# A new table of instruction orders for a fused attention, Fourier and feed-forward kernel

## The chip, the core and the metric

The kernel runs on one core of a Trainium2 chip. A core has four compute engines that run side by side, each its own list of instructions in order: TensorE (PE, with its weight loads PEld), VectorE (DVE), ScalarE (ACT) and GpSimd (POOL). SyncE (SP) issues the DMA transfers. An instruction waits until the semaphores of what it needs have come; what stands behind it on its engine waits too. The metric is the device time of one execution in microseconds (us).

## What is computed

Attention runs over 4 batches, 8 heads, 768 tokens of 64 values. A query sees only keys that belong to the same of 16 clusters as itself. The result goes through a two-dimensional Fourier transform, of which the real part is added, a normalisation, and a feed-forward layer of width 2048.

```python
q_assign = np.argmax(np.einsum('bhsd,hcd->bhsc', q_n, c_n), axis=-1)
k_assign = np.argmax(np.einsum('bhsd,hcd->bhsc', k_n, c_n), axis=-1)
mask = q_assign[:, :, :, None] == k_assign[:, :, None, :]
scores = scale * np.matmul(q, k.transpose(0, 1, 3, 2))
scores = np.where(mask, scores, -1000000000.0)
scores = scores - np.max(scores, axis=-1, keepdims=True)
attn = np.exp(scores)
attn = attn / (np.sum(attn, axis=-1, keepdims=True) + 1e-09)
return np.matmul(attn, v).astype(np.float32)
...
x = np.ascontiguousarray(attn_out.transpose(0, 2, 1, 3)).reshape(B, S, H * D)
...
X = np.fft.fft(x, axis=1)
X = np.fft.fft(X, axis=2)
mixed = np.real(X).astype(np.float32)
u = x + mixed
mu = np.mean(u, axis=-1, keepdims=True)
var = np.mean((u - mu) ** 2, axis=-1, keepdims=True)
un = (u - mu) / np.sqrt(var + 1e-06)
ch = np.maximum(un @ w_ch1, 0.0) @ w_ch2
return (u + ch).astype(np.float32)
```

## The kernel before

Numbers are kept as pairs of 16-bit values, a high and a low part, so that one product takes three matmuls. The work is recorded in steps. A pair of heads (there are 16) has six steps of 128 queries; in a step each of the two heads has the following chain. PE forms the scores in a PSUM bank, `ps_big`, of which there are two, one a head (L538 for the first eight pairs, with the mask's matmuls L543 behind; L530 for the others). DVE scales them and takes the row's smallest negated value (L557). ACT takes the exponential (L560) and casts it to 16 bits (L568; in some steps POOL does, L566). POOL subtracts to get the low part (L569). SP transposes both parts with a DMA (L571) into the ring `pts`. Two steps later PE multiplies them with v (L589 to L591, `ps_o`), and DVE divides by the sums (L601, L603, L605). In the first pairs of batch 0 L557 writes to SBUF, so the bank is free when L557 ends; later it writes in place, and the bank is free when L560 ends.

Some steps ahead of its first score a pair is prepared: loads, the split of q and k (ACT L397, DVE L398) and of v (ACT L361, DVE L363), the matmuls with the cluster centres (L425, four column strips of 32), the choice of the cluster (ACT L428, PE L433, DVE L439, L441, L447 to L458) and the mask.

Beside the first batch the two weight matrices are read in 32 pieces, their largest value is found (L725, L728, L62 to L65) and they are split (ACT L744, L745, PE L754, DVE L758, ACT L764, L767, DVE L770 or POOL L768). When a batch's attention is done its Fourier transform follows: folds on DVE and POOL (L892, L915, L928), their split (ACT L897, DVE L899), matmuls (L991 and others), and then the feed-forward layer (up: L1286, ACT L1293 and L1294, POOL L1295; down: L1314, DVE L1318), beside the attention of the next batch.

What stands where on an engine is set by a table. The program is recorded, and at the end `Order.apply` takes each engine's instructions, unpacks that engine's string from `ORDERS`, which holds how far each instruction moves from the place where it was recorded, sorts by it and ties every instruction to the one before it. What an instruction needs from another engine it still waits for by semaphore, wherever it stands. The tables were found beforehand; the kernel itself decides nothing.

Of the kernel before, what the change touches and what calls it, by code (L numbers as in the profile page):

```python
# [32 lines left out]
SH = S // 2  # L33
# [34 lines left out]
class Counted:  # L68
# [5 lines left out]
    def tile(self, shape, dt, name, bufs=None, **kw):  # L74
# [28 lines left out]
    "SP": (
        "c-lRaX>J=a427wYW{I7xNl?@U3KT`}&=d5GJxcGApK*{P>1MaiOzp9U{Yc3f!&)fn@$r!gGHDR|^4Q6!gGNcRXRM{y8f(RG#j2I)UZV=Dz;DvE&Z"
        "WWjORwdi8OQ9sPI_8=M(##O%->&5qHOT~q3_u5Jj#}R?YEPA4chq_9KUBi0n3<K^hpo8a}SF!<2-Xt@~jn}8+|2fP0rphI*(I1g5Wi&;n-<L$hfw"
# [118 lines left out]
class Attention:  # L224
# [23 lines left out]
    VP = ()  # L248
# [1340 lines left out]
```

## Time and profile before

| what | value |
|---|---|
| timed runs | 949.96, 950.37, 955.26 us (median 950.37) |
| span of the profiled execution, first to last instruction | 949.3 us |
| PE busy | 863.9 us, 91% |
| DVE busy | 678.2 us, 71% |
| ACT busy | 601.6 us, 63% |
| POOL busy | 608.3 us, 64% |
| mean granted TensorE clock | 0.976 of 2.4 GHz |

The profile is one execution. Busy is the time in which an engine had an instruction running; a PE that is busy runs at the full clock of 2.4 GHz or at half of it, 1.2 GHz, which the clock column tells (1.00 is full). In the timeline a row is one instruction or a run of equal ones, with its start in us from the span's start, its duration, and, where the engine sat idle before it, for how long and what ended that. Names read out<-in; L557 is line 557 of the kernel before.

### The profile page before, as it was taken

The page shows a single profiled execution, that of the slowest core. Times are in us where ns is not written, and L with a number is a line of the kernel's source. Part 1 is how long each engine was busy: PE and PEld are TensorE (multiplying, and loading weights), DVE is VectorE, ACT ScalarE, POOL GpSimd, SP SyncE. Part 2 cuts the span into 40 slices and gives each one's busy share as a digit, 9 for nine tenths or more (in the row PEclk, how much of TensorE's full clock was granted, in tenths as well). Part 3 has the DMA queues.
Part 4 walks back from the last instruction along what each step waited for, and adds up shares of the span by engine and source line. Part 5 has one row for each costly group of instructions (what it writes and reads, how often), then busy time and mean ns, then how long its engine had stood idle before and what let it go on. Part 6 is the DMA issues. An engine that isn't in the chain of part 4 may idle for free.

```text
span 949.3 us, 23660 instructions
## 1 busy us (share of the span) xinstructions
PE 863.9 (91%) x9241; PEld 581.0 (61%) x9241; DVE 678.2 (71%) x1531; ACT 601.6 (63%) x944; POOL 608.3 (64%) x752
## 2 busy tenths in 40 slices
PE   4777776677999999998999999999999999999998
PEld 1334443345756748666758667667668586676674
DVE  7989888877756667677757567678773446889643
ACT  6989988776666747647757747657676563353320
POOL 3778786755876876746767768748677764342421
PEclk9999897889999999999999999999999999999999
DMA  9999999988588888999899889998887764201020
GB/s 360 242 217 192 233 262 222 224 169 159 103 169 144 146 178 164 184 177 173 157 171 184 174 155 187 197 173 187 151 147 153 132 118 101 60 1 41 19 78 23
DMA packets 405151, 150.20 MB, mean 158 GB/s; under 512 B 383024, under 2 KB 391728, under 8 KB 405040
## 3 DMA queue, kind: packets, MB, share of 16 engines
q1 hardware_dynamic: 404896, 148.67, 78.1%
q8 instruction: 72, 1.18, 0.5%
q14 instruction: 39, 0.32, 0.1%
q10 hardware_dynamic: 144, 0.03, 0.0%
HBM read 41.99 MB, written 6.29 MB: 51 GB/s over the span
## 4 chain that ended last, share of the span: by engine, by line
PE 56%; DMA 7%; DVE 5%; POOL 4%; ACT 4%; issue 2%; SPq 1%; ACTq 0%; POOLq 0%; DVEq 0%
PE ps_fb L1314 8%; PE ps_fc L1314 7%; DMA pts<-ph 7%; PE ps_fa L1286 6%; PE ps_fa L1314 5%; PE ps_fb L1286 5%; PE ps_fc L1286 5%; PE ps_big L530 5%; PE ps_big L1228 3%; POOL ph L569 2%; PE ps_o L589 2%; PE ps_o L590 2%; PE ps_o L591 2%; PE ps_big L538 1%; ACT ph L568 1%
## 5 line engine op out<-in xcount | busy, mean ns | idle before, releaser
L569 POOL TENSOR_TENSOR ph<-p,ph 128x768 f16<-128x768 f32 x144 | 238.4, 1656 | 112.8 <-ACT ph L568 96.8
L557 DVE TENSOR_SCALAR_CACHE_REDUCE ps_big<-ps_big,sce 128x768 f32<-128x768 f32 x144 | 145.4, 1020 | 60.5 <-PE ps_big L530 34.7
L1314 PEld LDWEIGHTS <-arena 128*128 128x128 f16 x1152 | 109.9, 98 | 121.4 <-issue 1.6
L560 ACT ACTIVATE p<-ps_big,rmx 128x768 f32<-128x768 f32 x144 | 128.7, 897 | 60.3 <-DVE ps_big L557 43.0
L568 ACT CAST ph<-p 128x768 f16<-128x768 f32 x144 | 119.6, 830 | 70.0 <-DMA pts<-ph 67.7
L1295 POOL TENSOR_TENSOR arena<-arena 128x256 f16<-128x256 f32 x160 | 110.8, 697 | 52.2 <-ACT arena L1294 51.6
L1286 PEld LDWEIGHTS <-w1h 128*128 128x128 f16 x1280 | 124.9, 98 | 17.9 <-issue 1.5
L589 PE MATMUL ps_o<-v,pts 128*128 128x66 f16 x1062 | 111.1, 194 | 3.9 <-DMA pts<-ph 2.1
L590 PE MATMUL ps_o<-v,pts 128*128 128x64 f16 x1062 | 110.3, 195 | 0.0
L591 PE MATMUL ps_o<-v,pts 128*128 128x66 f16 x1062 | 110.0, 193 | 0.0
L589 PEld LDWEIGHTS <-pts 128*128 128x128 f16 x1062 | 98.4, 97 | 13.7 <-issue 5.9
L590 PEld LDWEIGHTS <-pts 128*128 128x128 f16 x1062 | 98.4, 97 | 7.4 <-issue 2.6
L1314 PE MATMUL ps_fb<-w2h,arena 128*128 128x512 f16 x320 | 100.9, 379 | 0.0
L591 PEld LDWEIGHTS <-pts 128*128 128x128 f16 x1062 | 98.6, 99 | 0.4
L538 PE MATMUL ps_big<-u 64*128 64x384 f16 x576 | 71.7, 356 | 26.2 <-ACT p L560 13.0
L1286 PE MATMUL ps_fa<-arena,w1h 128*128 128x256 f16 x464 | 85.5, 273 | 0.0
L1314 PE MATMUL ps_fc<-w2h,arena 128*128 128x512 f16 x256 | 81.0, 379 | 0.3 <-ACT arena L1294 0.3
L1286 PE MATMUL ps_fb<-arena,w1h 128*128 128x256 f16 x424 | 78.3, 273 | 0.7 <-DVE arena L1056 0.4
L530 PE MATMUL ps_big<-u 96*128 96x384 f16 (+1 forms) x384 | 75.6, 325 | 2.4 <-ACT p L560 2.3
L1286 PE MATMUL ps_fc<-arena,w1h 128*128 128x256 f16 x392 | 72.4, 273 | 1.1 <-ACT arena L1294 1.1
L1286 PEld LDWEIGHTS <-w1l 128*128 128x128 f16 x640 | 62.5, 98 | 10.6 <-issue 1.6
L538 PEld LDWEIGHTS <-u 64*128 64x128 f16 x576 | 30.1, 100 | 54.3 <-issue 33.9
(371 smaller groups left out, 2149.2 us busy)
## 6 DMA issues: line engine op xcount, KB each, us to landing
arena<-in_moe_w_ch_dram SPq DMA_DIRECT2D x26, 512.0 KB, 5.6
scr<-in_k_dram SPq DMA_DIRECT2D x16, 384.0 KB, 4.3
scr<-in_q_dram SPq DMA_DIRECT2D x16, 384.0 KB, 4.2
vst<-in_v_dram SPq DMA_DIRECT2D x16, 384.0 KB, 4.1
out_dram<-arena SPq DMA_DIRECT2D x24, 256.0 KB, 2.8
u<-u SPq DMA_DIRECT2D x64, 96.0 KB, 2.7
u<-u SPq DMA_DIRECT2D x16, 192.0 KB, 3.2
pts<-ph SPq DMA_TRANSPOSE x161, 3.9
```

The costliest lines, as they stand in the source:

```text
L530: nc.tensor.matmul(out=ps[j][:, hf, 0:SH], lhsT=self.slots(x + 2 * j, 1)[0:n, sl], rhs=self.slots(y + 2 * j, 1)[0:n, hf * SH:(hf + 1) * SH ...
L538: nc.tensor.matmul(out=ps[j][:, hf, 0:SH], lhsT=hq[rows[j], a, sl], rhs=hk[rows[j], c, hs], start=(i == 0), stop=False)
L557: self.mark = nc.vector.tensor_scalar(out=ju, in0=ps[j][:, :, 0:SH], scalar1=ne, scalar2=None, op0=ALU.mult, op1=ALU.min, accum_out=m)
L560: nc.scalar.activation(x, ju, AF.Exp, bias=m, scale=-1.0)
L568: nc.scalar.copy(out=ph[:, 0], in_=p32)
L569: nc.gpsimd.tensor_tensor(out=ph[:, 1], in0=p32, in1=ph[:, 0], op=ALU.subtract)
L589: nc.tensor.matmul(out=o[:, at:at + W], lhsT=hi, rhs=v16[:, kt, 0:W], start=(kt == 0), stop=False)
L590: nc.tensor.matmul(out=o[:, at:at + D], lhsT=hi, rhs=v16[:, kt, 66:130], start=False, stop=False)
L591: nc.tensor.matmul(out=o[:, at:at + W], lhsT=lo, rhs=v16[:, kt, 0:W], start=False, stop=(kt == ST - 1))
L1286: nc.tensor.matmul(out=ps.rearrange("p (t x) -> p t x", x=P), lhsT=a[:, dc, fs], rhs=c[:, :, dc], start=(i == 0), stop=(i == 11))
L1295: nc.gpsimd.tensor_tensor(out=hl[:, f], in0=r, in1=hh[:, f], op=ALU.subtract)
L1314: nc.tensor.matmul(out=ps, lhsT=a[:, f, ts], rhs=w[:, f], start=(i == 0), stop=(i == 47))
```

## The change

All five strings of `ORDERS` (ACT, POOL, SP, DVE, PE) are replaced. The recorded program, its buffers and its arithmetic are the same; only the place of the instructions in the engines' lists differs, and with it which waits are needed. The new strings take 19 lines more, so a line of the kernel before has a number higher by 19 in the rows of the kernel after (L557 is L576, L538 is L557).

```diff
 ORDERS = {
     "Activation": (
-        "c-m!E*>2Q85G;?!dyx?3P=fM+1W16y|9=Hf@CG6h2qXyNNV4o{dz<R&@d9Ek+vAz(?&|95SpcZ8v&47ed(5w`ZLG6n#INSv8j#W8qxts{_td;w`%"
...
+        "c-l=>*=`y^5bT}Z;W9SZg2YOsBrkc&|Nl!A<&fe;KH>v|xx7H9y1Ey@g58<vqq@3!EYg#O?z9k*QnuQ~bE6Ba2Y9pHEIX}LczzAbEF(!$)8hfZ=diN(TCZ"
...
     ),
```

The first place is on PE, near the border of batch 0 and batch 1, about 154 us into the kernel before. `ps_fc_2777` takes the cluster matmuls of a pair that comes later, `ps_fb_2273` those of the weights, `ps_big_2524` and `ps_big_2525` the scores of the running pair's two heads, `ps_o_2071` its attention. Before, the cluster matmuls follow the weights, and the scores come behind all twelve of them:

```order
L754 MATMUL ps_fb_2273<-w2h_82,arena_67 128x512
L754 LDWEIGHTS arena_67
L754 MATMUL ps_fb_2273<-w2l_83,arena_67 128x512
L425 LDWEIGHTS ct_117
L425 MATMUL ps_fc_2777<-u_109,ct_117 32x384
L425 LDWEIGHTS ct_117
```

After, the last attention matmul and the mask's four (L562, was L543) of the same scores stand ahead of the cluster matmuls (L444, was L425):

```order
L610 LDWEIGHTS u_109
L610 MATMUL ps_o_2071<-v16_1667,u_109 128x66
L562 LDWEIGHTS u_109
L562 MATMUL ps_big_2524<-u_109 128x384
L562 LDWEIGHTS u_109
L562 MATMUL ps_big_2525<-u_109 128x384
L562 LDWEIGHTS u_109
L562 MATMUL ps_big_2524<-u_109 128x384
L562 LDWEIGHTS u_109
L562 MATMUL ps_big_2525<-u_109 128x384
L444 LDWEIGHTS ct_117
L444 MATMUL ps_fc_2777<-u_109,ct_117 32x384
```

The score block has moved ahead of the twelve cluster matmuls. It is also no longer in one piece: its first matmul (L557, was L538) now stands alone between attention matmuls (L608 to L610, were L589 to L591), many rows ahead of its second:

```order
L608 MATMUL ps_o_2071<-v16_1667,pts_110 128x66
L609 LDWEIGHTS pts_110
L609 MATMUL ps_o_2071<-v16_1667,pts_110 128x64
L557 LDWEIGHTS u_109
L557 MATMUL ps_big_2524<-u_109 128x384
L610 LDWEIGHTS pts_110
L610 MATMUL ps_o_2071<-v16_1667,pts_110 128x66
L608 LDWEIGHTS pts_110
L608 MATMUL ps_o_2071<-v16_1667,pts_110 128x66
```

Such single score matmuls between attention matmuls, and blocks cut in two to eight pieces, are found in most steps of the first eight pairs; before, a block of twelve stands in one piece as a rule.

The second place is on DVE, at the same time. `ps_big_2425` and `ps_big_2426` are the scores of the step before, whose banks the block above needs. Before:

```order
L557 TENSOR_SCALAR X1_64,rmx_2443<-ps_big_2425,sce_66 128x768
L626 TENSOR_SCALAR scp_65<-ps_fc_2477 128x3
L770 SCALAR_TENSOR_TENSOR w2l_83<-ps_fa_2065,wsc_2060,w2h_82 128x512
L627 RECIPROCAL scp_65<-scp_65 128x3
L899 SCALAR_TENSOR_TENSOR arena_67<-arena_67,vseq_2243 128x3x64 x2
L601 TENSOR_SCALAR rs_2316<-ps_o_2071,scp_65 128x6
L758 SCALAR_TENSOR_TENSOR ps_fa_2266<-arena_67,ps_fa_2266 128x512
L758 SCALAR_TENSOR_TENSOR ps_fb_2273<-arena_67,ps_fb_2273 128x512
L915 TENSOR_TENSOR arena_67<-X0_63 128x765
L398 SCALAR_TENSOR_TENSOR u_109<-scr_2155,scp_65,u_109 128x768 x2
L603 RECIPROCAL rs_2316<-rs_2316 128x6
L557 TENSOR_SCALAR X1_64,rmx_2450<-ps_big_2426,sce_66 128x768
```

After (L576 was L557, L934 was L915, L911 was L892, L777 was L758, L417 was L398, L645, L789 and L646 were L626, L770 and L627):

```order
L934 TENSOR_TENSOR arena_67<-X0_63 128x765
L642 TENSOR_SCALAR ps_fc_2477<-ps_fc_2477 128x3
L645 TENSOR_SCALAR scp_65<-ps_fc_2477 128x3
L789 SCALAR_TENSOR_TENSOR w2l_83<-ps_fa_2065,wsc_2060,w2h_82 128x512
L646 RECIPROCAL scp_65<-scp_65 128x3
L911 TENSOR_TENSOR arena_67<-arena_67 128x3x127
L576 TENSOR_SCALAR X1_64,rmx_2443<-ps_big_2425,sce_66 128x768
L576 TENSOR_SCALAR X1_64,rmx_2450<-ps_big_2426,sce_66 128x768
L777 SCALAR_TENSOR_TENSOR ps_fa_2266<-arena_67,ps_fa_2266 128x512
L777 SCALAR_TENSOR_TENSOR ps_fb_2273<-arena_67,ps_fb_2273 128x512
```

The two reductions follow each other now; L892 has come ahead of them, L915 (and L899, whose rows end a little above) has stayed ahead of the second, and the two L758 and L398 stand behind.

The third place is on ACT, about 180 us into the kernel before. `p32_2629` and `p32_2637` are the exponentials of one step's two heads. Before:

```order
L560 ACTIVATE p32_2629<-ps_big_2610,rmx_2628 128x768
L767 ACTIVATE arena_67<-ps_fa_2559,wsc_2376 128x512
L568 CAST ph_2632<-p32_2629 128x768
L897 ACTIVATE arena_67<-arena_67,vseq_2243 128x6x64
L744 ACTIVATE w2h_82<-arena_67 128x1024
L560 ACTIVATE p32_2637<-ps_big_2611,rmx_2636 128x768
L745 ACTIVATE w2l_83<-arena_67 128x1024 x2
```

After (L579 was L560, L587 was L568, L916 was L897, L763 was L744):

```order
L579 ACTIVATE p32_2629<-ps_big_2610,rmx_2628 128x768
L587 CAST ph_2632<-p32_2629 128x768
L579 ACTIVATE p32_2637<-ps_big_2611,rmx_2636 128x768
L916 ACTIVATE arena_67<-arena_67,vseq_2243 128x6x64
L763 ACTIVATE w2h_82<-arena_67 128x1024
```

The second head's exponential now follows the first head's cast; the split L897 and the weights' L744 and the cast of the weights' sums (L767) no longer stand between.

## Rows read from the trace of the kernel before

**Rows 1.** Page, section 1: busy us, share of the span, instructions.
```profile
span 949.3 us, 23660 instructions
...
PE 863.9 (91%) x9241; PEld 581.0 (61%) x9241; DVE 678.2 (71%) x1531; ACT 601.6 (63%) x944; POOL 608.3 (64%) x752
```

**Rows 2.** Windows: us of stretch, busy us by engine, PE clock, DMA share, GB/s.
```profile
0.00:232.00 232.00, 159.79 (x1941) 89.11 (x1941) 200.63 (x443) 188.99 (x251) 159.04 (x191) 0.90 1.04 231
232.00:949.00 717.00, 704.15 (x7304) 491.85 (x7300) 477.58 (x1088) 412.62 (x693) 449.26 (x562) 1.00 0.71 135
```

**Rows 3.** Waits, 0 to 232 us: engine, line, waited for; total us, times, longest.
```profile
ACT ac L428 <- PE ps_fc L425: 3.5, 2, 3.1
...
ACT arena L960 <- PE ps_fb L991: 0.2, 1, 0.2
```

**Rows 4.** Timeline of PE: start, us, instruction, [idle before and releaser].
```profile
160.67 0.51 PE L425 MATMUL ps_fc<-u,ct 128*32 128x384 f16 x4 [3.91 <-DVE u L398]
161.12 2.66 PE L538 MATMUL ps_big<-u 64*128 64x384 f16 x12
```

**Rows 5.** Timeline of DVE, 150 to 162 us.
```profile
150.83 1.02 DVE L557 TENSOR_SCALAR_CACHE_REDUCE X<-ps_big,sce 128x768 f32<-128x768 f32 x1 [1.00 <-POOL ph L569]
...
153.19 2.14 DVE L899 SCALAR_TENSOR_TENSOR arena<-arena,vseq 128x192 f16<-128x192 f32 x2 [0.53 <-ACT arena L897]
...
155.38 0.68 DVE L758 SCALAR_TENSOR_TENSOR ps_fa<-arena,ps_fa 128x512 uint32<-128x512 uint32 x1
155.98 0.68 DVE L758 SCALAR_TENSOR_TENSOR ps_fb<-arena,ps_fb 128x512 uint32<-128x512 uint32 x1
156.58 2.18 DVE L915 TENSOR_TENSOR arena<-X 128x765 f32<-128x765 f32 x1
158.68 1.94 DVE L398 SCALAR_TENSOR_TENSOR u<-scr,scp,u 128x768 f16<-128x768 f32 x2
...
160.64 0.97 DVE L557 TENSOR_SCALAR_CACHE_REDUCE X<-ps_big,sce 128x768 f32<-128x768 f32 x1
...
161.54 0.55 DVE L892 TENSOR_TENSOR arena<-arena 128x381 f32<-128x381 f32 x1
```

**Rows 6.** Timeline of PE, 179 to 186 us.
```profile
179.14 0.32 PE L538 MATMUL ps_big<-u 64*128 64x384 f16 x1 [2.18 <-ACT p L560]
183.61 2.08 PE L538 MATMUL ps_big<-u 64*128 64x384 f16 x11 [4.15 <-ACT p L560]
```

**Rows 7.** Timeline of ACT, 180 to 184 us.
```profile
180.30 0.83 ACT L568 CAST ph<-p 128x768 f16<-128x768 f32 x1 [0.63 <-DMA pts<-ph]
...
181.58 1.19 ACT L744 ACTIVATE w2h<-arena 128x1024 int16<-128x1024 int16 x1
182.67 0.89 ACT L560 ACTIVATE p<-ps_big,rmx 128x768 f32<-128x768 f32 x1
```

**Rows 8.** Timeline of DVE, 179 to 184 us.
```profile
179.97 1.02 DVE L557 TENSOR_SCALAR_CACHE_REDUCE ps_big<-ps_big,sce 128x768 f32<-128x768 f32 x1
...
181.56 1.75 DVE L363 SCALAR_TENSOR_TENSOR v<-vst,scp,v 128x384 f16<-128x384 f32 x1
```

**Rows 9.** Source lines, 25 to 200 us: count, ns min/median/max, first and last start.
```profile
L363 DVE SCALAR_TENSOR_TENSOR v<-vst,scp,v x10: 607/1155/2000, 55.1 to 181.6; 128x384 f16<-128x384 f32 x10
...
L899 DVE SCALAR_TENSOR_TENSOR arena<-arena,vseq x8: 406/413/1802, 153.2 to 190.9; 128x192 f16<-128x192 f32 x8
```

**Rows 10.** Groups by line: count, busy us, mean ns, idle before.
```profile
L363 DVE SCALAR_TENSOR_TENSOR v<-vst,scp,v 128x384 f16<-128x384 f32 x10 | 12.0, 1213 | 0.0
...
L569 POOL TENSOR_TENSOR ph<-p,ph 128x768 f16<-128x768 f32 x144 | 238.4, 1656 | 112.8 <-ACT ph L568 96.8
```

**Rows 11.** Timeline of PE, 343 to 345 us, at full clock.
```profile
343.43 0.38 PE L1314 MATMUL ps_fb<-w2l,arena 128*128 128x512 f16 x1
343.65 0.38 PE L1314 MATMUL ps_fb<-w2h,arena 128*128 128x512 f16 x1
343.96 1.15 PE L538 MATMUL ps_big<-u 64*128 64x384 f16 x12
```

More of the change, by code (lines that the diff above doesn't have):

```diff
@@ new lines @@
+        "+$VQIZK)uJ3!@8Az=swzCeeB7S$&%Me;Vjc8kBse?6VGE<{-HUEmrtU_@MZDN`2RJ-9*k;_Wn%3m^)7}*#p*|8baaR=*)tH(gyV?Pttwr_Q|r9tgkR_LzH"
+        "U*fc^bbv^0`kD$qLo?Qkuj)Kk#8OjvU3S$zr!tLx*(`T3WetZV|BR6twbY3&d6a@!E9_p%4Jx?`)W%1qUSDWa^4%Ce1Hu#Zw>aY4^yccD>TZA1iPJgx9H8"
+        "EfHuG2RwVZ-UQ)(Z!B`xfJk-f%BDj_ja5uM5Gh@h&(svFf<N84n=@p>IL%Zs=XmdKhJ=asr|Q3)9}wIX`v?@}9mw*$vYU0XGfn&M3b8FpXfN4!77=M!t`$"
+        "ai(6RiXM!iy3#fnD*=FT?;Y0^ejT(S$xJ9)J)z_S~}A37_)PWPW)1@)$Z>$t!I1Y`eb8>t_)x+p}Q1kUhAVCrnncg^P=9PR;&-7#Cvpu+w4v=Ynw;+9AD-"
@@ new lines @@
+        "qpj`LHDN-n5a)SJoZH!?nA}vQuqF58Ld>H#sn=$44?PH?(!H%&fVdvgRHorRYxa)BY>!F;R?(yRzxnknvEh_AMnN?y-iI?3z_<HN6mLEON%Akj;?YQ(4-g"
+        ">#cVg0`F4Vt}i-pi(bdfYru*tqH_mN42=#Z#-cC^diy1cTfkB!%FxiCfPY1%DCVl&BeOQQMNxi;*R;KAY^qp|Yw_{_V5sPMtHHILRGf4EC$f*1^2qA&?DD"
+        "SNqXe4YRE9XW`&SXO#41#~O`Q#+1DCk=)V`D2V)tlKV8r#5Y%O{A(0Vv0YdxM?U5UK}6MG#L(^HA8Kj(&cV2pA=Z~9sSq7L_oN<{`dpk<$DhMb?-$=GhOx"
+        "04Nd;uyb@xJB5ZYm%VP?ap_hdOZ`m1#&B=&&$TO$dH3E9d-i)51TeWXUt2<tI(6UWmt6ap1Jl!C3+Lj46C^@(zV(M{|{#zf}!cio{0Di_*HJi)}7!xL2Z?"
@@ L102 @@
+        "6WXj-`@h6AA7W$TrB<S>?*c+{0Yhy#G<1Z03?HB"
     ),
     "SP": (
[L104 to L107 removed]
@@ new lines @@
+        "7y?~YfMcRjbHireDQ=T+kwqbUe;y{KN~{EBRagI}BS-jf;<{3YXjucJJUxz+v#<%g+lkI#qjrIagoWf&8D-j->TO|XDv&OT|DR>fOX*`7rBN1AdJ8P+7`N"
+        "JOvNGJ!%$FW$iGqJD00G{PZ{q)^Kb;)-O94Y(ybx<kG9&`*boMX^KqTqewp$~Pr3jayPk1@p9{e%I+G%&x=RI4uo+)$B{JoRYfssIB~sx*xzz$xWt8jp}`"
+        "dBfO`K_%trdc|-kAN;X7eiHT1~T8z*m>afo&Y;%5;tHAjR$6k!i6&vP9l{ULFVv^g2**9`H;Hoi=<2pwd7)8X(;WK%jF*sfca{;bybEe>>^6T_&gTCokSN"
+        "3HL_Xkvg4*giC%~|>|j7waR*_xN!T7Q`tjJdK$+dfy3*(i@L^&Y3^DZY>unc>Pl*GIhP^l8Z6bkzz+ALe^v9>pB*T9*CUq|6WeR{tIi_~^<wtp17jF{u2w"
@@ new lines @@
+        "%|^kx<Cs=~W<24uO6?u$U$G2Fn8O8}r0*$bff=Z0BlK!hZcw6Ws27YttIwH?<|*aa349{QsmH-*CZ{jE5?e)0@J+`xl9mjhU?u37)@v5J2Y4T6<TCBoSj*"
+        "~1Y<Neki5jaeqb-f0#&vTX|6BT@cVdgFf<?wYWS;Gcb|6fHYHG2kHl=QH`qQE8Vc>=6YOze|F>2luUu~MneMthk>Suy)Wr{Uax3SF7*13c|=;(10^l2s%`"
+        "aEoJ1*@_xr8SM<NB2tqL;BRU+;${8P#wT2yeW@a&LYEG(N37F9kVvdy7*d-nXX@`qj3Py%pz}vegF|G^W>|bPkF^cqbsW^BWg>0USh`<vM!Y{9vdzh$L_W"
+        "0oK;hY`AQ92k5b!E2WxsSVB42fYDrl)RmM{Zo<y8~24}_Bdq<r0%%U-aVxpPpSR}flVvN}|?6m_b@C>J44$tB{(RGv5<vG-uHzydw2yNCwWvZR$@Da5nl&"
@@ L151 @@
+        "at<`N%o?EU*$*Rx8?*AI-T#2#7D}yuGlIVF(aH4M3Mn+{^z65JJHJM$j)#IhPnk}`c8B#aP+0vM8mut9PDO1a2|CI6GOXa*uR*#oCZcH>gCi_l{+O0M8pM"
+        ")lKciW2<y>2JqSz2RTR>4o_J#EJ3-x{7V8;*Z1&(?kO(#Y`+51g@QoS}d*eYn%}WdS^@d*F-$B3~cwD?FLxau3a`uFvhC6VXi9U`S<DX~G&J+ii)veou2E"
+        "7hS{{8&F<6FlQ^5Z!>tVkmJmf_wq9bdZnkcr4?fJPt)uFw}6Y&"
     ),
```

119 lines of the change are left out of this document (60 added, 59 removed).

## Prediction

> **What bounds the kernel now.** I read the busy lines first: PE works in 91% of the span of 949.3 us, DVE in 71% [rows 1]. An average over the span hides that there are two stages, so next I cut the span in two [rows 2]. From 232 us to the end PE is busy 704.15 of 717 us at clock 1.00: here PE is the bound, and an order can win at most the 12.85 us in which PE is not busy. In the first 232 us PE is busy 159.79 us only, its clock is 0.90 on the mean, DVE is busy 200.63 us, ACT 188.99, and the DMA engines always (share 1.04). No single engine is the bound there; the chain passes from one to the other, and what is lost is lost in waits. PE is idle 232 - 159.79 = 72.2 us there, more than five times as long as later. So the question is how long the first stage lasts: the PE work behind it is the same in both orders, and each microsecond by which the first stage gets shorter for the same PE work moves the end.
>
> The waits on PE tell which way the chain runs in the first stage. The other engines wait for PE 22.8 us in all, in 17 rows, of which the first and the last stand in [rows 3]; that is 22.8 / 232 = 10% of the stage. PE waits far more for them than they for it. I use this 10% below as the share of a change in PE's own time that reaches the end of the stage.
>
> The two longest stretches without matmuls come next. Up to 160.67 us PE's queue holds the cluster matmuls of a coming pair (L425), which wait for DVE's split L398; behind them stand 12 score matmuls of the running pair, which start at 161.12 [rows 4]. DVE meanwhile works through L899, L758, L915 and L398 before it comes to the second reduction (L557, at 160.64) that empties the score bank [rows 5]. At 179 us a score block starts with one matmul, and its second waits 4.15 us for ACT's exponential [rows 6]; that exponential stands on ACT behind L897 and L744 and starts at 182.67 [rows 7], though the reduction that feeds it was done at 179.97 + 1.02 = 180.99 [rows 8].
>
> **The change, part by part.** Nothing is added or removed; every term below is a wait that moves. I take the two places where the order shows a clear edit, then three costs that are spread over the first stage.
>
> *The place at 154 us.* On PE the score matmuls of the running pair now stand ahead of L425, so what starts them is the bank alone, that is the end of the second L557. On DVE that L557 now stands right behind the first one; L758 twice (0.68 + 0.68) and L398 twice (1.94) come behind it, L892 (0.55) comes ahead, and L899 and L915 stay ahead of it. It ended at 160.64 + 0.97 = 161.61 [rows 5]; with 3.30 us taken from ahead of it and 0.55 put there, less some 0.15 of overlap, it ends 2.6 us earlier. That is the lower bound. L899 took 2.14 us for two where its median is 0.413 [rows 9], so 1.31 us of it were a wait; DVE also sat idle 1.00 us before the first L557 and 0.53 before L899 [rows 5]. If all of these go in the new neighbourhood, 2.8 us more are won: 5.4. I take 4.0, between the two, since each of these waits may come back elsewhere. L425 is late by the same score block; the pair that it prepares is not the running one, so several score blocks cover it. Without that cover the score blocks of that pair would wait for it as before.
>
> *The place at 179 us.* On ACT the exponential now stands right behind the cast L568, which ended at 180.30 + 0.83 = 181.13 [rows 7], so it starts about 181.05 instead of 182.67: 1.6 us, and the 11 score matmuls behind it likewise. The bound below is nothing, if the cast itself comes later (it waited 0.63 us for a transfer). L897 and L744 are late by the one exponential instead; what DVE does with L897's output is covered by a split of v of 1.75 us [rows 8].
>
> *DVE waiting for GpSimd.* The split of v, L363, takes 0.607 us at the least and up to 2.000 [rows 9]. Over 25 to 200 us ten of them take 12.0 us [rows 10], so 12.0 - 6.07 = 5.9 us are such waits, for this one line; the new order can take them away or double them: bounds -5.9 and +5.9. The edits that I see take the split at 181.56 out to a later place and L899 to another one; I take a third off, 1.9 us.
>
> By the Trainium skill, page "SBUF — State Buffer", section "SBUF: two separate sides", the port pair of the two engines is an exclusive lock that is held for a whole instruction. The spread of L363 agrees with that; by the rule alone ten such splits would, with POOL busy 159.04 of 232 us [rows 2] and half of a GpSimd subtraction of 1656 ns [rows 10] to wait each, lose an estimated 5.7 us, which is what the rows show: the old order does not avoid such meetings, and one that does would win up to 5.9.
>
> *More shapes on PE.* The score matmuls of the first eight pairs use half the array's rows (64*128) and run in pairs side by side. In the old order their 48 blocks of 12 stand in 55 runs, in the new one in 122, with attention matmuls of full height between. I counted in both orders how often consecutive matmuls differ in the array shape: 222 times before, 362 now, 140 more, nearly all in the first stage. Two matmuls of L1314 start 343.65 - 343.43 = 0.22 us apart, and the score block behind them starts 343.96 - 343.65 = 0.31 us after the second: the switch costs 0.09, say 0.10 us [rows 11]. 140 x 0.10 = 14.0. A broken pair costs a slot: 12 in a block take 1.15 us [rows 11], about 0.17 a pair when the tail of the last is left out, and in the new order I count some 30 pairs torn apart: 30 x 0.17 = 5.0. So PE has 19.0 us more to do, bounds 0 and 19.0; much of it lies where PE waited anyway (the single matmul with 4.15 us behind it is such a place). By the 10% of above I take 1.9 us of loss.
>
> The page "TensorEngine Tiling (Array Packing)", section "Key Properties", of the Trainium skill says that changing the tiling mode drains the engine, which speaks against this order. The page "TensorE: Matmul & The Clock Gate", section "Single matmul latency", puts a drain at about 175 ns; by that the 140 switches would be an estimated 24.5 us rather than 14.0, and the loss about 3 us rather than 1.9.
>
> *PE's clock.* In the first stage the mean clock is 0.90, so of 159.79 us busy some 16.0 are lost to the lower level, 1.2 instead of 2.4 GHz [rows 2]. It shows after waits: the 11 score matmuls behind the 4.15 us took 2.08 us [rows 6], where 12 take 1.15 at full clock [rows 11]. Bounds 0 and 16.0; by the same 10%, 1.6 us of gain.
>
> *Behind 232 us.* Blocks move within PE's order, producers with them. PE is not busy for 717 - 704.15 = 12.85 us there [rows 2], and the two producers that it would wait for, ACT and DVE, are busy 58% and 67% of that time. The bounds are that these 12.85 us go or double; I take no change, since nothing in the order that I read says which.
>
> **The sum.** 949.3 - 4.0 - 1.6 - 1.9 + 1.9 - 1.6 = 942.1 us of span. The median of the three runs is 950.37, 1.07 above the profiled span: **943.2 us**, 0.8% faster. With the first two terms at their bounds and the third at nothing or twice its value the forecast's own range is 939 to 948.
>
> **The rivals.**
> - *The stage is held by the transfers.* The DMA engines are busy in a share of 1.04 of the first 232 us [rows 2], and both orders move the same bytes. Then what is won at 154 and 179 us is waited for at the hand-over to the feed-forward: 950.4 us, no change. Against it: the longest waits of PE above end on DVE and ACT, not on a transfer. Chance 0.23.
> - *PE stays at full clock.* The attention matmuls between the score matmuls fill just the holes after which the clock fell. If all of the 16.0 us come back, not 1.6: 942.1 - 14.4 + 1.07 = 928.8 us. For it: the holes are many, and filling them costs little. Against: a quicker PE shortens the stage only where something waits for it, 10% of it. Chance 0.19.
> - *The shapes cost in full; slower.* If all 19.0 us lie on the chain, since the score block is what DVE and ACT wait for next: 942.1 - 1.9 + 19.0 + 1.07 = 960.3 us. The other terms are worth 9.1 us, so it is slower than before from 9.1 / 19.0 = 48% on the chain. For it: attention matmuls stand inside score blocks also where the bank may be free. Against: the 10%. Chance 0.10.
>
> **How the numbers follow.** The forecast has chance 0.48. One per cent, 9.5 us, is about what a measurement here can tell from no change. Faster by over 1%, under 940.9: the clock rival, 0.19, and the lower part of the forecast's own range, 0.18: 0.37. Slower, over 959.9: the part of the last rival with nearly all 19.0 us on the chain, 0.05, and 0.04 for idle time behind 232 us that nearly doubles on top of a first stage without gain: 0.09. The rest, 0.54, is within 1%. The range leaves one in ten out on either side: 931 to 957.
>
> **What would show it.** Right: in the profile after L425 no longer holds score matmuls back near 154 us and the second L557 follows the first at once; PE busy in the first stage rises by up to 19.0 us, the dense stage begins 5 to 9 us earlier and stays at 98%. Wrong: a dense stage with new waits of PE on ACT or DVE, a first stage as long as before with a DMA share over 1, or score blocks that end late, with waits for PE far above 22.8 us.

## The result, and the profile of the changed kernel

| | before | changed |
|---|---|---|
| timed runs | 949.75 to 955.26 us, median 950.16 | 963.91 to 965.98 us, median 964.55 |
| ratio, 95% interval | | 1.0138 [1.0111, 1.0166] |
| span of the profiled execution | 949.3 us | 963.8 us |

The changed kernel is 1.4% slower, where 0.8% faster was forecast, and 7.6 us above the range. The page's head and first section, and the windows that answer [rows 1, 2] (columns as there):

```profile
span 963.8 us, 23679 instructions
...
PE 883.3 (92%) x9241; PEld 585.9 (61%) x9241; DVE 679.5 (71%) x1531; ACT 603.5 (63%) x944; POOL 612.5 (64%) x752
```

```profile
0.00:232.00 232.00, 176.01 (x1964) 94.36 (x1964) 197.91 (x447) 188.54 (x250) 161.91 (x190) 0.93 1.05 231
232.00:963.80 731.80, 707.28 (x7280) 491.55 (x7277) 481.61 (x1085) 415.00 (x694) 450.54 (x562) 1.00 0.68 132
```

In the first 232 us PE is busy 16.2 us more than before. Behind them it is not busy for 731.80 - 707.28 = 24.5 us, where it was 12.85. To see which of the two stages moved the end, I line the traces up by PE's progress: the columns of its matmuls, in its own order, summed as time at 2.4 GHz. The first column is that sum, the second the time at which the kernel before had come so far, and the others how much later (+) or earlier (-) the other kernels had; e1, e2, e4 and e10 are experiments below.

```
PE work  before   changed   e1     e2     e4     e10
   24      41.3     +3.6   -0.6   +3.3    0.0   +4.0
   88     122.1     -1.7   +0.8   -1.6   -1.5   -0.9
  112     150.9     +4.8   +0.8   +4.2   +3.2   +6.1
  120     166.6     +0.3   +0.5   -0.1   -3.2   +0.4
  136     198.2     -1.8   +1.3   -1.8   -6.3   -1.5
  168     238.3     -0.9   +0.6   -1.9   -1.7   -1.8
  232     294.4     -1.6   +1.9   -0.5   -1.7   -2.5
  320     373.8     +4.9   +6.8   -0.4   -1.9   -2.2
  420     481.6     +8.3  +10.2   +0.7   -1.3   -6.1
  580     649.0    +10.0  +14.1   +1.7   -0.1  -11.3
  740     815.4    +14.5  +18.2   +1.4   +1.1  -11.1
  860     938.7    +14.2  +17.9   +1.4   +1.1  -11.4
```

At one sum the two orders have not done the same work, so rows of the first stage move by some us for that reason alone; later they settle. The first stage ends 0.9 us earlier, not 7.2. The loss comes behind it, in the stage for which no change was forecast: from -1.6 us at 294 us to +14.5 at 815, in many steps. The waits of PE behind 250 us in the changed kernel (engine, line, waited for: total us, times, longest), of which the first and some others stand here:

```profile
PE ps_big L549 <- ACT p L579: 3.0, 4, 1.6
PE ps_o L608 <- DMA pts<-ph: 2.9, 3, 2.4
PE ps_fa L1010 <- ACT arena L1066: 2.1, 1, 2.1
PE ps_fa L50 <- ACT arena L1074: 1.9, 1, 1.9
PE ps_fa L1305 <- ACT arena L1313: 1.2, 2, 0.8
...
PE ps_fc L452 <- ACT ac L447: 0.2, 1, 0.2
```

The score banks that wait for the exponential were at the head of this list before, too:

```profile
PE ps_big L530 <- ACT p L560: 2.3, 5, 0.7
```

What is new is how many other waits there are, none of them over 2.4 us. The longest shows what such a wait can hang on. The changed kernel, 348 to 362 us:

```profile
348.27 0.84 SPq L371 DMA_DIRECT2D vst<-in_v_dram  x1
...
349.69 0.38 SPq L391 DMA_DIRECT2D scr<-in_q_dram  x1
...
350.13 0.42 SPq L391 DMA_DIRECT2D scr<-in_k_dram  x1
...
351.41 1.44 SPq L590 DMA_TRANSPOSE pts<-ph  x1
...
359.33 0.24 PE L608 MATMUL ps_o<-v,pts 128*128 128x66 f16 x1 [2.35 <-DMA pts<-ph]
359.36 0.83 ACT L587 CAST ph<-p 128x768 f16<-128x768 f32 x1 [2.08 <-DMA pts<-ph]
...
360.27 3.23 POOL L588 TENSOR_TENSOR ph<-p,ph 128x768 f16<-128x768 f32 x2 [3.69 <-ACT ph L587]
```

One late transposing transfer, issued at 351.41 behind three loads of a coming pair, holds three engines: PE, which needs its output; ACT, whose next cast needs its buffer; and POOL, which needs the cast. From its issue to its landing it took (DMA view, 351 to 353 us):

```profile
pts<-ph SPq DMA_TRANSPOSE x1, 7.9
```

The median of such transfers is 3.8 us (below). The ring of cast L568, subtraction L569, transfer L571 and next cast (lines of before) has two buffers, `ph`, from the fifth pair on; it is what the experiments came down to.

For the sums below I split each trace by hand: gaps (PE without a matmul for over 0.15 us), changes of the array's shape with the time over the columns' own that they cost, and the time in which the clock was at 1.2 GHz.

```
            first 250 us: gaps, changes, their cost, time at 1.2 GHz | behind: gaps
before             64.8     134       22.9         44.4              |    8.6
changed            48.8     277       43.3         34.1              |   19.7
e1                 61.7     134       23.9         61.4              |   23.4
e2                 46.6     277       40.9         37.5              |   11.3
e3                 57.5     134       23.9         58.0              |   12.9
```

### The profile page after: what moved, and what is told of

The parts are those of the page before. It is cut to its first block, busy times and chain, and to the rows that moved or that the text cites. A ratio compares the mean times of both kernels' runs of the same rounds, so it can differ in the third digit from the quotient of the medians.

```text
span 963.8 us, 23679 instructions
## 1 busy us (share of the span) xinstructions
PE 883.3 (92%) x9241; PEld 585.9 (61%) x9241; DVE 679.5 (71%) x1531; ACT 603.5 (63%) x944; POOL 612.5 (64%) x752
## 4 chain that ended last, share of the span: by engine, by line
PE 49%; DMA 20%; ACT 9%; DVE 8%; POOL 7%; issue 4%; SPq 2%; ACTq 0%; POOLq 0%; DVEq 0%
DMA pts<-ph 15%; PE ps_fb L1333 7%; PE ps_fc L1333 6%; PE ps_fa L1333 6%; PE ps_fa L1305 5%; PE ps_fb L1305 4%; PE ps_fc L1305 4%; POOL ph L588 4%; PE ps_big L549 3%; PE ps_big L1247 3%; PE ps_big L557 3%; ACT ph L587 2%; PE ps_o L608 2%; PE ps_o L610 2%; PE ps_o L609 1%
## 5 line engine op out<-in xcount | busy, mean ns | idle before, releaser
L576 DVE TENSOR_SCALAR_CACHE_REDUCE ps_big<-ps_big,sce 128x768 f32<-128x768 f32 x144 | 146.0, 1020 | 76.2 <-PE ps_big L549 47.7
L587 ACT CAST ph<-p 128x768 f16<-128x768 f32 x144 | 119.3, 830 | 90.5 <-DMA pts<-ph 86.5
L579 ACT ACTIVATE p<-ps_big,rmx 128x768 f32<-128x768 f32 x144 | 129.2, 899 | 61.2 <-DVE ps_big L576 24.5
L1333 PEld LDWEIGHTS <-arena 128*128 128x128 f16 x1152 | 102.2, 98 | 87.3 <-issue 4.1
L608 PE MATMUL ps_o<-v,pts 128*128 128x66 f16 x1062 | 141.9, 195 | 12.2 <-DMA pts<-ph 8.9
L609 PE MATMUL ps_o<-v,pts 128*128 128x64 f16 x1062 | 141.2, 195 | 0.0
L610 PE MATMUL ps_o<-v,pts 128*128 128x66 f16 x1062 | 141.0, 194 | 0.0
L608 PEld LDWEIGHTS <-pts 128*128 128x128 f16 x1062 | 101.0, 98 | 38.3 <-DMA pts<-ph 11.3
L610 PEld LDWEIGHTS <-pts 128*128 128x128 f16 x1062 | 100.9, 99 | 28.3 <-issue 12.6
L609 PEld LDWEIGHTS <-pts 128*128 128x128 f16 x1062 | 100.5, 98 | 27.4 <-issue 14.9
L1333 PE MATMUL ps_fb<-w2h,arena 128*128 128x512 f16 x320 | 110.6, 379 | 0.0
L557 PE MATMUL ps_big<-u 64*128 64x384 f16 x576 | 81.0, 349 | 17.0 <-DVE X L576 12.9
L549 PE MATMUL ps_big<-u 128*128 128x384 f16 (+1 forms) x384 | 88.6, 325 | 5.8 <-ACT p L579 3.0
L1305 PE MATMUL ps_fa<-arena,w1h 128*128 128x256 f16 x464 | 92.5, 272 | 1.2 <-ACT arena L1313 1.2
L1333 PE MATMUL ps_fc<-w2h,arena 128*128 128x512 f16 x256 | 89.7, 383 | 0.0
L1333 PE MATMUL ps_fa<-w2h,arena 128*128 128x512 f16 x192 | 66.9, 379 | 0.0
```

Source lines behind the costliest of these rows:

```text
L549: nc.tensor.matmul(out=ps[j][:, hf, 0:SH], lhsT=self.slots(x + 2 * j, 1)[0:n, sl], rhs=self.slots(y + 2 * j, 1)[0:n, hf * SH:(hf + 1) * SH ...
L557: nc.tensor.matmul(out=ps[j][:, hf, 0:SH], lhsT=hq[rows[j], a, sl], rhs=hk[rows[j], c, hs], start=(i == 0), stop=False)
L576: self.mark = nc.vector.tensor_scalar(out=ju, in0=ps[j][:, :, 0:SH], scalar1=ne, scalar2=None, op0=ALU.mult, op1=ALU.min, accum_out=m)
L579: nc.scalar.activation(x, ju, AF.Exp, bias=m, scale=-1.0)
L587: nc.scalar.copy(out=ph[:, 0], in_=p32)
L608: nc.tensor.matmul(out=o[:, at:at + W], lhsT=hi, rhs=v16[:, kt, 0:W], start=(kt == 0), stop=False)
```

## Experiments: which stage

The order of an engine is a list, and two orders can be joined at a moment of the trace: what had started by then follows the one, the rest the other. The strings are packed, so the edit is told in words here:

```diff
 ORDERS = {
-    "PE": old list,
+    "PE": old list of what had started by 250 us, then new list of the rest,
...
```

**e1, old head and new tail.**

> Each engine follows the old order for all that the kernel before had started by 250 us, and the new order for everything else. Theory T (the tail's own waits: the new order behind 250 us makes PE wait for producers that the old one had ready): PE's idle gaps over 0.15 us rise from 8.6 to some 20 us behind 250 us and the time is 950.2 + 16 = 966 us. Rival H (the hand-over: the new first stage leaves the producers behind, and the order of the tail is harmless): 950 us.

Measured: 967.01 us, ratio 1.0168 [1.0135, 1.0202].

**e2, new head and old tail.**

> The mirror: the new order for all that the changed kernel had started by 250 us, the old order behind it. Theory T: the time is that of before less the 1.5 us by which the new first stage ends earlier, 948.7 us. Rival H: 950.2 + 14 = 964 us.

Measured: 953.93 us, ratio 1.0027 [1.0014, 1.0041]. The windows from 250 to 850 us of before, changed, e1 and e2:

```profile
250.00:850.00 600.00, 590.75 (x6145) 413.58 (x6142) 402.14 (x905) 373.32 (x622) 411.19 (x490) 1.00 0.80 152
```

```profile
250.00:850.00 600.00, 579.68 (x6014) 402.69 (x6013) 393.59 (x882) 366.97 (x605) 403.88 (x487) 0.99 0.79 152
```

```profile
250.00:850.00 600.00, 576.11 (x6012) 400.68 (x6011) 391.25 (x881) 364.18 (x601) 400.84 (x478) 1.00 0.79 152
```

```profile
250.00:850.00 600.00, 588.39 (x6105) 411.46 (x6104) 397.15 (x893) 372.64 (x620) 411.27 (x489) 1.00 0.81 152
```

With the new tail PE gets through some 130 matmuls fewer in these 600 us, whichever head stands ahead, and e1 goes the way of the changed kernel in the progress table, 2 to 4 us behind it. Theory T holds and the hand-over falls, though e2 is 5.2 us above theory T's figure: the new head by itself brings nothing, and the joined order is 0.3% slower than the one before.

**e16, new from 250 to 430 us only.**

> The old order, except that what stands between 250 us of before and 430 us of after follows the new order. Theory A (the loss is a sum of many single places): it has the part that the changed kernel lost by there, about 7 of 15.7 us: 957 us. Rival B (an order fits as a whole, and each seam costs): 965 us or more.

Measured: 961.83 us, ratio 1.0118 [1.0081, 1.0154], between the two. Its trace lacks 20 of the 9241 matmuls, all of the first 200 us, 4.3 us by their columns. With these added it was 2.8 us earlier than before at 238 us and 4.2 later at 417, so it lost 7.0 us in the window, as theory A says, and another 4.5 between 425 and 435, at the seam, where the old order has to go on from a state that is not its own. The part of the loss that belongs to these 180 us comes with them; the rest comes later, so no single place makes it all.

## Experiments: the first stage

**e3, new head with whole score blocks.** Of one score block on PE near 154 us, - in the new order, + in e3 (lines of before):

```diff
-L538 MATMUL ps_big_2524<-u_109 128x384
-L591 MATMUL ps_o_2071<-v16_1667,pts_110 128x66
...
+L538 MATMUL ps_big_2524<-u_109 128x384
+L538 MATMUL ps_big_2525<-u_109 128x384
```

> As the kernel with the new order to 250 us and the old one behind it, but on PE the 12 score matmuls of a step stand in one piece again, at the place of the last of them: 222 changes of the array's shape in the whole program, as before the change. Theory S (the added changes of shape, 20.4 us of PE's time in the first stage, are on the path and have eaten what the waits won): the stage ends 5 to 15 us earlier, 934 to 944 us. Rival F (they only fill holes in which PE would wait): the holes come back, 946 to 951 us.

Measured: 954.19 us, ratio 1.0036 [1.0014, 1.0058], the same as e2. The shapes cost what they were priced at: in the changed kernel 43.3 - 22.9 = 20.4 us for 143 changes more, 0.14 us each with the torn pairs in it. Taking them out gave 40.9 - 23.9 = 17.0 us back, and gaps (46.6 to 57.5) and time at the lower clock (37.5 to 58.0 us) took it again. The windows of the first 232 us of e2 and e3:

```profile
0.00:232.00 232.00, 178.22 (x1973) 97.29 (x1974) 200.02 (x451) 189.24 (x250) 161.56 (x190) 0.92 1.06 231
```

```profile
0.00:232.00 232.00, 168.84 (x1958) 95.43 (x1959) 194.77 (x446) 188.19 (x250) 161.49 (x190) 0.87 1.06 230
```

PE is busy 9.4 us less for nearly as many matmuls, and the stage is no shorter. Theory F's reading holds, at a time 3 us above its figure: the shapes fill holes, and so does a lower clock.

**e4, the two places alone.** The old lists, with the new ones between 146 and 196 us.

> The old order, except that what stands between 146 us of before and 196 us of after follows the new order: the two places at 154 and 179 us alone. Theory P (the two edits are worth what the prediction said, 4.0 + 1.6 us): 950.2 - 5.6 = 944.6 us. Rival B (what is won there is waited for again before the dense stage begins, as something else sets its start): 950 us.

Measured: 953.71 us, ratio 1.0027 [1.001, 1.0045]. By its progress it was 1.5 us ahead at 122 us, ahead of the window, and 6.3 at 198: 4.8 us for the two places, where 5.6 were forecast. Of the 6.3, 3.3 went at once, into a wait of the Fourier transform for the weights' split that the window's end had left late (timeline of PE in e4):

```profile
196.65 0.81 PE L991 MATMUL ps_fb<-arena 128*128 128x129 f16 x6 [3.31 <-ACT arena L767]
```

Rival B is nearer the truth. In the changed kernel, too, the first place was faster (from +4.8 to +0.3 us), and 6.5 us were lost between 122 and 151 us of before (from -1.7 to +4.8).

**e11 and e12, what holds this stage.**

```diff
-            nc.sync.dma_start(out=pt, in_=ph.rearrange("p a x -> p (a x)"), transpose=True)
+            nc.sync.dma_start(out=pt[:, 0:ST] if 1 < 2 * pr + st // 3 and pr < 5 else pt, in_=ph[:, 0] if 1 < 2 * pr + st // 3 and pr < 5 else ph.rearrange("p a x -> p (a x)"), transpose=True)
```

> The kernel before, with the transposing transfers of the first five pairs (but for the first steps) cut to the high halves, 768 of 1536 columns; PE multiplies what the buffers held before. Theory D (the transfers hold the first stage, whose DMA share is 1.04): the dense stage begins 8 us earlier or more, 942 us or less. Rival K (the chain through the engines holds it): 947 to 952 us.

```diff
+            f, h = ph.rearrange("p a x -> p (a x)"), S // 2 if 2 * pr + st // 3 > 1 and pr < 5 else S
...
-                nc.scalar.copy(out=ph[:, 0], in_=p32)
-            nc.gpsimd.tensor_tensor(out=ph[:, 1], in0=p32, in1=ph[:, 0], op=ALU.subtract)
-            nc.sync.dma_start(out=pt, in_=ph.rearrange("p a x -> p (a x)"), transpose=True)
+                nc.scalar.copy(out=f[:, 0:h], in_=p32[:, 0:h])
+            nc.gpsimd.tensor_tensor(out=f[:, h:2 * h], in0=p32[:, 0:h], in1=f[:, 0:h], op=ALU.subtract)
+            nc.sync.dma_start(out=pt[:, 0:2 * h // P], in_=f[:, 0:2 * h], transpose=True)
```

> The kernel before, with cast, subtraction and transfer of the first five pairs (but for the first steps) cut to half. It takes as many bytes from the transfers as the run with half the transfers, and also some 20 us from ACT and 40 us from POOL. Theory D: the same time as that run. Theory K (ACT, DVE and POOL hold the first stage): at least 8 us less than that run, 942 us or less. Rival W (neither; the stage is held by DVE and the order alone): 947 to 952 us.

Measured: e11 951.38 us, ratio 0.9993 [0.997, 1.0017]; e12 945.23 us, 0.9917 [0.989, 0.9945]. The first 232 us of each:

```profile
0.00:232.00 232.00, 162.17 (x1965) 91.55 (x1966) 200.21 (x446) 189.15 (x251) 157.67 (x191) 0.90 0.80 190
```

```profile
0.00:232.00 232.00, 167.65 (x1995) 95.10 (x1996) 197.74 (x451) 179.90 (x257) 122.22 (x193) 0.89 0.81 192
```

The DMA share fell from 1.04 to 0.80 and the time did not move: the transfers do not hold this stage. With 9 us less of ACT and 37 us less of POOL in it, the dense stage began 4.6 us earlier in the trace, and e12 is 6.2 us faster than e11, where theory K asked 8. So ACT's and POOL's time is a part of what holds the stage. DVE, busy 195 to 201 of 232 us in all of these kernels, was not shortened, so what holds the rest stays open.

## Experiments: what the new tail waits for

**e5 and e6, one engine's list from the other order.** In words again, for e5:

```diff
 ORDERS = {
-    "PE": old list,
+    "PE": old list to 250 us, then new list,
...
```

> The old order, except that from 250 us on PE alone follows the new one (99 instructions of the other engines, mostly DVE's and ACT's, are brought forward by a few places each, as the new order of PE needs them earlier). Theory Q (PE's own new order takes the work up too early): 962 to 967 us. Rival R (the new orders of ACT, DVE, POOL and SP deliver later): 950 to 954 us. Rival M (neither is bad alone; each list is fitted to its own partners): this kernel and its mirror are both above 960 us.

> The mirror: the old order, except that from 250 us on ACT, DVE, POOL and SP follow the new one and PE the old (40 instructions brought forward). Theory Q: 950 to 954 us. Rival R: 962 to 967 us. Rival M: above 960 us.

Measured: e5 1247.3 us, ratio 1.3117 [1.3065, 1.3169]; e6 1146.59 us, 1.2061 [1.2027, 1.2095]. The first wait of PE behind 250 us in each:

```profile
PE ps_big L530 <- ACT p L560: 52.9, 23, 6.0
```

```profile
PE ps_big L530 <- ACT p L560: 33.6, 20, 3.3
```

Rival M, far beyond its figure: here five lists are one order. Which engine's list is at fault is then no question that a mixture answers.

**e7 and e8, the waiting matmuls later.** PE's list alone: a matmul that waited, and what needs it, stands behind the independent ones that followed it.

The first of e8's edits, on PE at 397 us (weight loads left out):

```diff
 L1314 MATMUL ps_fb_5979<-w2l_83,arena_67 128x512
+L1314 MATMUL ps_fb_5979<-w2h_82,arena_67 128x512
...
 L991 MATMUL ps_fa_6218<-arena_67 128x129
...
-L1314 MATMUL ps_fb_5979<-w2h_82,arena_67 128x512
```

> The changed kernel's order, with 19 edits on PE alone: where its trace shows PE idle for more than 0.25 us behind 250 us (18.1 us in all), the matmuls that waited, with those that need them, stand behind 0.6 to 2.9 us of the independent matmuls that followed. Theory L (each of these waits is one reader that stands too early by that much, while later work is ready): at least half of the 18.1 us goes, 955 us or less. Rival C (work is short everywhere; the wait moves to the next reader): 961 to 965 us.

> The order of the kernel before, with 13 edits of the same kind on PE, at its own gaps of over 0.25 us behind 250 us (8.0 us in all). Theory L: half of them goes, 946 us. Rival C: 949 to 952 us.

Measured: e7 973.49 us, ratio 1.0232 [1.0204, 1.0259], where the changed kernel has 1.0138; e8 962.48 us, 1.0115 [1.0081, 1.015]. The gaps behind 250 us grew, from 19.7 to 24.3 us and from 8.6 to 17.0. Theory L falls, and rival C was too mild. My reading, which no run shows, is that many of these matmuls stand at the head of a chain that comes back to PE: put later, they make their own successors late.

**e9 and e10, a shorter ring.** The edit of e12, for the pairs from the seventh on.

> The kernel before, with half the work left out between the exponential and the attention matmuls of the pairs from the seventh on (the cast, the subtraction and the transposing transfer take 384 columns instead of 768; PE's own work is the same, and the attention of these pairs is not the reference's). It shows what shorter producers are worth behind 260 us with the old order, where PE's gaps over 0.15 us are 8.6 us: 944 to 949 us.

> The same half work in the changed kernel. Theory N (the new order behind 250 us runs PE too close behind its producers, so it waits whenever they are a little late; with shorter producers most of its extra waits go): 950 to 956 us, and the distance to the old order with the same work falls from 14 to under 8 us. Rival V (the loss has nothing to do with how fast these producers are): the distance stays at 12 to 16 us, 957 to 964 us.

Measured: e9 941.65 us, ratio 0.9883 [0.9846, 0.992]; e10 941.2 us, 0.988 [0.9841, 0.9918]. The distance between the orders goes from 14.4 us (964.55 - 950.16) to nothing, more than theory N asked, and both times lie below the ranges expected; PE's gaps behind 250 us are 3.9 and 3.2 us. The waits of PE there in e10, six in all:

```profile
PE ps_fc L1010 <- DMA arena<-in_ss_dram: 0.8, 1, 0.8
PE ps_fc L1010 <- DVE scp L648: 0.7, 1, 0.7
PE ps_fa L1027 <- DVE arena L981: 0.6, 1, 0.6
...
PE ps_fb L1010 <- DVE arena L1337: 0.2, 1, 0.2
```

**e13, e14 and e15, which part of the ring.** e13 and e14 have the edit of e11 from the seventh pair on (so the transfer also no longer waits for the subtraction). e15:

```diff
-            nc.gpsimd.tensor_tensor(out=ph[:, 1], in0=p32, in1=ph[:, 0], op=ALU.subtract)
-            nc.sync.dma_start(out=pt, in_=ph.rearrange("p a x -> p (a x)"), transpose=True)
+            h = S // 2 if pr > 5 else S; nc.gpsimd.tensor_tensor(out=ph[:, 1, 0:h], in0=p32[:, 0:h], in1=ph[:, 0, 0:h], op=ALU.subtract)
+            nc.sync.dma_start(out=pt[:, 0:(S + h) // P], in_=ph.rearrange("p a x -> p (a x)")[:, 0:S + h], transpose=True)
```

> The changed kernel, with only the transfers of the pairs from the seventh on cut to the high halves (768 of 1536 columns; PE multiplies what the buffers held before for the low halves). Theory X (the new order runs too close to the transfers, which the cast and the next subtraction wait for when buffers come free late): 948 to 954 us, most of what the half chain took back. Rival Y (ACT's and POOL's own time): 960 to 965 us.

> The same half transfers in the kernel before, as the control: 946 to 951 us if the transfers matter (theory X), 950 to 952 us if not (rival Y).

> The changed kernel, with POOL's subtraction of the pairs from the seventh on cut to 384 of 768 columns (0.8 us less each) and the transfer to 1152 of 1536. Theory X: about half of what the half transfers take back, 955 to 960 us. Rival Y in POOL: 945 to 952 us. Rival Y in ACT's cast: 962 us or more.

Measured: e13 944.44 us, ratio 0.9928 [0.9908, 0.9947]; e14 945.53 us, 0.9956 [0.9936, 0.9975]; e15 944.84 us, 0.9942 [0.9922, 0.9961]. The waits of ACT's cast for the transfer, 250 to 850 us, in before, changed, e14, e13 and e15:

```profile
ACT ph L568 <- DMA pts<-ph: 65.9, 52, 3.8
```

```profile
ACT ph L587 <- DMA pts<-ph: 79.6, 50, 5.4
```

```profile
ACT ph L568 <- DMA pts<-ph: 15.8, 15, 2.1
```

```profile
ACT ph L587 <- DMA pts<-ph: 19.6, 14, 3.6
```

```profile
ACT ph L587 <- DMA pts<-ph: 41.5, 25, 4.5
```

The median transfer from issue to landing, 480 to 860 us (group, times, us at the end), in changed, e15 and e13:

```profile
pts<-ph SPq DMA_TRANSPOSE x76, 3.8
```

```profile
pts<-ph SPq DMA_TRANSPOSE x72, 3.3
```

```profile
pts<-ph SPq DMA_TRANSPOSE x72, 2.8
```

The exponential's wait for the subtraction, the ring's other wait on ACT (it needs the buffer that the subtraction reads), in before, changed, e13 and e15, 250 to 850 us:

```profile
ACT p L560 <- POOL ph L569: 6.5, 9, 1.4
```

```profile
ACT p L579 <- POOL ph L588: 19.3, 18, 3.9
```

```profile
ACT p L579 <- POOL ph L588: 20.5, 18, 4.0
```

```profile
ACT p L579 <- POOL ph L588: 6.7, 5, 4.1
```

In e15 the transfer is 0.5 us and the subtraction 0.8 us shorter, 1.3 us a turn, and the ratio to before falls from 1.0138 to 0.9942, by 19 us; e13 wins as much. In the old order the half transfers are worth 5 us. e13 speaks against rival Y, but e15 came out 10 us below theory X's figure, at that of rival Y in POOL. The two agree if the ring as a whole is too long, whichever of its parts is cut: e13 takes 60.0 us from the cast's wait and nothing from the exponential's, e15 38.1 and 12.6. Which part counts for more is not separated. Nor is a rival that neither text names: both runs also take bytes off the DMA engines, whose share over 250 to 850 us falls from 0.79 to 0.57 and 0.69.

**e17 and e18, the same with nothing left out.**

```diff
-            nc.sync.dma_start(out=pt, in_=ph.rearrange("p a x -> p (a x)"), transpose=True)
+            for o, i in ([(pt[:, a * ST:(a + 1) * ST], ph[:, a]) for a in (0, 1)] if pr > 5 else [(pt, ph.rearrange("p a x -> p (a x)"))]): nc.sync.dma_start(out=o, in_=i, transpose=True)
```

> The changed kernel, computing everything; in the pairs from the seventh on a transfer is cut in two, the high halves behind the cast and the low halves behind the subtraction (120 more issues on SP, each right ahead of the one it was part of; the same bytes). Theory Z (what the new order runs too close to is the end of the transfer, which comes earlier when only half of it is left behind the subtraction): 946 to 956 us. Rival S (SP's time for an issue, 1.4 us each, or the latency of a transfer whatever its size eats it): 962 us or more.

> The same two transfers in the kernel before. Theory Z: 945 to 949 us, less than both kernels. Rival S: 951 us or more.

Measured: e17 994.17 us, ratio 1.0401 [1.0341, 1.0462]; e18 981.83 us, 1.0283 [1.022, 1.0345]. Rival S. In e18, 480 to 860 us (issues of L571, ns min/median/max; the cast's wait; a transfer's landing):

```profile
L571 SPq DMA_TRANSPOSE pts<-ph x152: 1209/1232/2564, 480.8 to 810.7; - x152
...
  ACT ph L568: 71.3, 40
```

```profile
pts<-ph SPq DMA_TRANSPOSE x152, 2.8
```

The cast's wait in the kernel before, same window:

```profile
  ACT ph L568: 43.2, 32
```

A half lands 2.8 us after its issue, where the whole took 3.8, and an issue holds SP for 1.23 us, so the low halves come no earlier (1.23 + 2.8 = 4.0) and the cast waits 71.3 us where it waited 43.2. By the three sizes a transfer is an estimated 1.8 us plus 1.0 for each half. The Trainium skill says the like: on the page "DMA: Bandwidth & Descriptors", section "Anatomy of one DMA — SWDGE (gpsimd) path", about 2.0 us of a transfer are fixed, most of it until the end is confirmed. These transfers are issued by SP, so the agreement is with the size only. None of the versions that compute everything beat the kernel before.

## Why the prediction was wrong

**The step that failed** is the one on the stage behind 232 us: "I take no change, since nothing in the order that I read says which." The idle 12.85 us became 24.5, its upper bound to within 1.2 us, and PE was busy 3.1 us more, about the 3.4 us that 6.8 us at 1.2 GHz cost, where there had been none. e1 and e2 put the whole loss there. The bound stood in the text, but the chance of "nearly doubles on top of a first stage without gain" was put at 0.04; both halves came true. So did the text's signs of being wrong: new waits of PE on ACT in the dense stage, and a first stage as long as before at a DMA share of 1.05. I had read from [rows 2] that ACT and DVE were busy 58% and 67% there, and took that for reserve. It was none here: the ring has two buffers, and with a microsecond or so less in a turn the new order lost nothing (e10, e13, e15). The row that could be read beforehand is the cast's wait for the transfer, 65.9 us over 52 times, in the trace of before; it says that the ring is tight, though not that a new order will lose by it. Moving single matmuls on PE does not cure the loss (e7), and the mixtures (e5, e6) could not say which list makes it.

What in the new order makes the ring late no run tests, but the traces show one part of it. SP's new list issues the loads of q and k (384 KB each) within 1.0 us of each other for all nine pairs loaded behind 250 us; in the old list they stand 3.6 to 23.4 us apart for seven of the nine. In both kernels a transposing transfer without a load of q, k or v in the 3 us ahead of it lands 3.8 us after its issue (median). Behind two or three such loads it is 5.2 us before, a single case, and in the changed kernel 3.8 to 7.9, seven cases. The two latest of these were issued at 291.2 and 351.4 us and took 7.5 and 7.9 us, where the same transfers had taken 3.8 and 4.4; e1 (7.9, 6.4) and e16 (7.3, 7.9), with the new order there, repeat it, and e2 with the old one does not (3.8, 4.5). At these two places (294 to 310 and 350 to 358 us of before) the changed kernel falls behind by 2.1 and 3.1 us, of some 16 behind 250 us, and e1 by 2.5 and 0.2, so this is a part and not the whole. With half transfers behind the same loads (e10) they took 4.1 and 5.4 us, and no time was lost there. The rest of what makes the new order less tolerant stays open.

**The place at 154 us** was right on DVE. DVE's two reductions stand 0.94 us apart (157.10 - 156.16), where they stood 9.8 apart [rows 5]:

```profile
156.16 1.00 DVE L576 TENSOR_SCALAR_CACHE_REDUCE X<-ps_big,sce 128x768 f32<-128x768 f32 x1
...
157.10 1.01 DVE L576 TENSOR_SCALAR_CACHE_REDUCE X<-ps_big,sce 128x768 f32<-128x768 f32 x1
```

The progress table gives 4.5 us for it, where the forecast was 4.0, but the same order had lost 6.5 us just ahead of it. A smaller wait took the place of L425's 3.91 [rows 4], the mask's matmuls for their transfer:

```profile
163.71 0.34 PE L562 MATMUL ps_big<-u 32*128 32x384 bf16 x4 [2.00 <-DMA u<-oh]
```

**The place at 179 us** went to its lower bound, for the reason given there: the cast came later. The exponential stands right behind it, but the cast waited 1.80 us for a transfer, so the exponential started at 183.59 us instead of 182.67, and PE's hole of 4.15 us [rows 6] stayed, with another name:

```profile
182.85 0.83 ACT L587 CAST ph<-p 128x768 f16<-128x768 f32 x1 [1.80 <-DMA pts<-ph]
183.59 0.89 ACT L579 ACTIVATE p<-ps_big,rmx 128x768 f32<-128x768 f32 x1
```

```profile
182.82 0.24 PE L608 MATMUL ps_o<-v,pts 128*128 128x66 f16 x1 [4.07 <-DMA pts<-ph]
...
184.54 2.07 PE L557 MATMUL ps_big<-u 64*128 64x384 f16 x11 [0.51 <-ACT p L579]
```

**DVE waiting for GpSimd** went nearly to its bound. The splits of v, 25 to 200 us (answer to [rows 10]; count | busy us, mean ns):

```profile
L382 DVE SCALAR_TENSOR_TENSOR v<-vst,scp,v 128x384 f16<-128x384 f32 x9 | 6.6, 743 | 0.9 <-ACT v L380 0.9
```

Nine of them take 6.6 us, 1.2 over their shortest, where ten had taken 5.9 over: for this line the new order does keep the two engines apart. By the Trainium skill's page "SBUF — State Buffer", section "SBUF: two separate sides", this is the exclusive lock met less often; the trace agrees. But the stage was not shorter for it, so the term of 1.9 us was no gain in time.

**Shapes and clock.** The price of the shapes was 20.4 us where 19.0 were counted, 0.14 us a change where [rows 11] had given 0.10 and the torn pairs were counted apart. The Trainium skill's page "TensorE: Matmul & The Clock Gate", section "Single matmul latency", has about 0.175 us for a drain; the trace stays below it. The share of 10% that reaches the end was too high: e3 shows 0. (The 22.8 us behind that share are 16 rows of other engines; the 17th is PE's own weight load, 0.2 us.) The same for the clock: 34.1 us at 1.2 GHz instead of 44.4, and no gain. The sum of the first stage, -7.2 us, came out at -0.9.

**The rivals.** The slower one came nearest in time (960.3) by the wrong way: the first stage did not get longer, and whole blocks (e3) did not make it shorter. "Transfers hold the stage" gave no gain there, as it happened, but e11 shows that they do not hold it. It is behind 250 us, at a DMA share of 0.8, that halving them took the loss away (e13).

## What to carry to other kernels

An order that is set by hand or by search has to be judged also where PE is 98% busy: each wait there is lost for good, and a low load on the other engines said nothing here about the ring of buffers that feeds PE. Look for the wait of a producer for its own buffer (here a cast for its transfer), shorten that ring by a microsecond in an experiment, and see how far the time moves; one run for each order (e13, e14) told how much it depends on the ring. Then look at what the list of the DMA queue puts right ahead of the ring's transfers. Filling holes with work, or making the work in them quicker, moved nothing here.

## What the runs showed of the hardware that I had not expected

A transposing transfer of 128x768 16-bit values took 2.8 us from issue to landing, one of 128x1152 3.3 and one of 128x1536 3.8 (medians), so by estimate one more transfer costs 1.8 us of latency, and it held SP for 1.23 us. Right behind loads of 384 KB each, one of 128x1536 took up to 7.9 us. A change of the array's shape with torn pairs in it cost 0.14 us. And in e3 the time at the lower clock rose by 20.5 us when PE had less to do, without the stage getting longer.
